# State products of a unit issued ahead of its score products, and the state sum taken in the same unit

## Chip, cores and metric

The kernel runs on one core of one Trainium2 chip. The metric is device time in microseconds of one execution. A core has five engines with queues of their own that run in order: TensorE (PE in the profile, with its weight loads listed as PEld), VectorE (DVE), ScalarE (ACT), GpSimd (POOL) and SyncE (SP, which here only starts DMAs).

## The reference, cut to what matters

A gated recurrence over 768 steps for 4 batches and 8 heads of width 40, followed by a mixture of 16 experts. Only the recurrence bears on this change:

```python
for t in range(S):
    m_new = np.maximum(f_gate[:, :, t] + m, i_gate[:, :, t])
    f_stab = np.exp(f_gate[:, :, t] + m - m_new)
    i_stab = np.exp(i_gate[:, :, t] - m_new)
    m = m_new
    C = f_stab * C + i_stab * outer(v_t, k_t)      # state, per batch and head 40 x 40
    n = f_stab * n + i_stab * k_t
    h_tilde = C @ q_t
    y[:, :, t] = sigmoid(o_t) * h_tilde / max(|n . q_t|, 1)
# then: x = y as rows of 320; a group and an expert chosen per row; out = weight * relu(x w1) w2
```

## The kernel before, in words

**Units.** The recurrence is done in chunks of 128 steps. A unit `u` is one batch in one chunk: `c, b = divmod(u, 4)`, 24 units in all, six chunks. Within a unit the outputs are a sum of two parts: the part from inside the chunk (scores of keys against queries, weighted by a decay, times values) and the part carried in from earlier chunks (queries times the state `Cst`). The state of a batch is kept in SBUF, as four pairs of heads with 41 columns each (40 of the value and one for the normalizer), in `Cst` (also seen as `Cflat`).

**The steps of a unit and their engines:**

- `scores` (L212, PE): 8 products into the two score banks `sp`, in row tiles of 64 and 40 partitions.
- `masked` (L217, DVE): scores times decay, twice, into `pt`.
- `carried` (L237, PE): 8 products of queries and `Cflat` into the tile `it`; nothing in the first chunk. `it` is two banks of PSUM and there is only one buffer of it, so the tile of one unit is given out once all readers of the last unit's are done.
- `carried2` (L244, DVE): reads that part out of `it` into `num`.
- `decayed` (L263, POOL): multiplies the batch's state by the decay of the chunk. Not in the first and last chunk.
- `values` (L284, PE): 8 products of `pt` and the values into `av`.
- `state` (L256, PE): 8 products of weighted keys `kw` and the values, 41 columns each, in column tiles of 64, into the second bank of `it`. Not in the last chunk (units 20 to 23).
- `state2` (L271, in the first chunk L273; DVE): adds these into `Cst`, or copies them.
- `keyw` (L224, POOL): makes `kw` of the next unit from its keys and the last column of its decay.
- `decay` (L182, L185 on PE into `aw`, then four exponentials L195 on ACT into `ab`), in two halves for the unit after the next; `mask` (L166, POOL) of the next unit's decay.
- `norm1`, `rows` (L290 to L300, DVE), `rows2` (L306, POOL), `turn` (L314 on PE, L334 on ACT), `store` (a DMA on SP): normalize the last unit's output, transpose it and store it.

**The order.** Up to unit 21 the order of instructions on each engine is that of the program, written out by hand in `unit(u)`; from unit 22 on a planner orders them by its own costs. In `unit(u)` the small steps of the routing ("chores", `route`, L381 to L452) and the splitting of the first expert's weights into two parts (L651 on ACT, L653 on DVE) are strewn into the later half of a unit. Units with `u % 4 == 0` and `u > 0` also carry the routing logits of the last chunk (`logits_of`, L363 and L368 on PE, L365 on ACT between them), behind `values` and `state`.

The start is written out as well: unit 0 step by step, then `unit(1, first=True)`, in which both halves of the decay of unit 2 follow the scores of unit 1. `gate_sums(1)` (L899 to L923) prepares the gates of the second chunk, mostly on DVE; three steps of it run within unit 0 and the rest behind unit 1. `ends` (L935 on PE, L938 on ACT) follows unit 2; `gate_o` (L163, ACT) is a long activation in units 2, 6, 10 and so on.

Of the kernel before, what the change touches and what calls it, by code (L numbers as in the profile page):

```python
# [7 lines left out]
F32 = mybir.dt.float32  # L8
# [10 lines left out]
P = 128  # L19
# [13 lines left out]
D1 = D + 1  # L33
Z = 64 - D
KS = 64 + D
HC = 4 * D1
# [17 lines left out]
def bc(ap, shape):  # L54
    return ap.broadcast_to(list(shape))
# [3 lines left out]
def lstm_moe(ctx: ExitStack, tc: tile.TileContext, gates, qkT, nat, og, wcat, w1, w2, cst, out):  # L59
    nc = tc.nc  # L60
    enter = ctx.enter_context
    mm = nc.tensor.matmul
# [55 lines left out]
    ps_a = att.enter_context(tc.tile_pool(name="ps_a", bufs=1, space=PSUM))  # L118
# [28 lines left out]
    st_ = {}  # L147
# [9 lines left out]
    def load_o(c):  # L157
        t = wk.tile([P, B, DM], F32, name="sig")
        nc.sync.dma_start(t, og[:, c * B:(c + 1) * B, :])
        sigs[c] = t  # L160
# [36 lines left out]
    def decay(u, r, **kw):  # L197
        aprod(u, r, **kw)
        exps(u, r)
# [14 lines left out]
    def masked(u, r):  # L214
        t = st_[u]
        pt = wk.tile([P, 4, P], F32, name="pt", bufs=4)
        nc.vector.tensor_tensor(pt, t["pm"][r], t["ab"][:, r], op=ALU.mult)  # L217
        t["pm"][r] = pt

    def keyw(u):  # L220
        t = st_[u]
        if u // B < NCH - 1:
# [2 lines left out]
                                    t["nt"][:, DM + H:].rearrange("p (j r d) -> p r j d", r=2, d=D),  # L225
                                    bc(t["ab"][:, :, :, P - 1:P], (P, 2, 4, D)), op=ALU.mult)

    def carried(u):
        c, b = divmod(u, B)
        t = st_[u]  # L230
        it = t["it"] = ps_a.tile([P, 2, 512], F32, name="it")
        if c > 0:
            for pr in range(4):
                for r in range(2):
                    rs = rows_of[r]
                    o = (b * 4 + pr) * D1
                    mm(it[:, r, pr * D1:pr * D1 + P], t["qk"][rs, 1, pr, :], Cflat[rs, o:o + P], start=True, stop=True)  # L237
# [11 lines left out]
    def state(u):  # L249
        c, b = divmod(u, B)  # L250
        t = st_[u]
        nt = t["nt"]
        if c < NCH - 1:
            for j in range(H):
                pr, r0 = j // 2, 64 * (j % 2)
                mm(t["it"][r0:r0 + 64, 1, HC + pr * D1:HC + (pr + 1) * D1], t["kw"][:, pr * KS + r0:pr * KS + r0 + 64],  # L256
                   nt[:, j * D1:(j + 1) * D1], start=True, stop=True)

    def decayed(u):
# [5 lines left out]
    def state2(u):  # L265
        c, b = divmod(u, B)
        if c < NCH - 1:
            st = st_[u]["it"][:, 1, HC:2 * HC].rearrange("p (a e) -> p a e", e=D1)
            cb = Cst[:, b * 4:b * 4 + 4, :]
            if c > 0:  # L270
                nc.vector.tensor_tensor(cb, cb, st, op=ALU.add)  # L271
            else:
                nc.vector.tensor_copy(cb, st)  # L273
# [93 lines left out]
    def logits_back(c):  # L367
        nc.tensor.transpose(out=rt["bank"][:, 0:P], in_=rt["lT"], identity=ident)  # L368
        chores.append([route(c, 0, B, rt["bank"]), "B"])
# [85 lines left out]
    def go_on(n=1, slot=None):  # L455
        while n and chores and slot in (None, chores[0][1]):
            n -= 1
            with ExitStack() as st:
                if not rt["manual"]:
                    st.enter_context(tc.high_priority())  # L460
                chores[0][1] = next(chores[0][0], None)
                if chores[0][1] is None:
                    chores.pop(0)
# [17 lines left out]
    def first_tokens():  # L481
        none = rt["rows"][0]
        nc.sync.dma_start(itab[0:NE * NBLK, :].rearrange("(p a) b -> p (a b)", p=P), none)
        nc.sync.dma_start(itab[NE * NBLK:NE * NBLK + 1, :], none[0:1, 0:P])

    def last_rows():
        zero = rt["rows"][1]
        for b in range(B):
            nc.sync.dma_start(x_d[b * S + S - P:(b + 1) * S, :], zero)
        nc.sync.dma_start(x_d[NTOK:NTOK + 1, :], zero[0:1])  # L490

    def put_id():
        if ids:
            sl, tk = ids.pop(0)
            nc.gpsimd.memset(sep, 0.0)
            no_order("ids", nc.gpsimd.indirect_dma_start(  # L496
                out=itab_flat, out_offset=bass.IndirectOffsetOnAxis(ap=sl, axis=0), in_=tk, in_offset=None))
# [324 lines left out]
    def run(stage, u):  # L822
        if 0 <= u < NU:
            stage(u)
# [12 lines left out]
    def unit(u, more=0, first=False):  # L837
        run(loads, u + 3)
        if u == 6:
            first_tokens()  # L840
        if u == 9:
            last_rows()
        if u % B == 1 and u // B + 1 < NCH:
            load_o(u // B + 1)
        with ExitStack() as st:
            if u == MANUAL:
                st.enter_context(tc.issue_after(rt["av", u - 1].ins))
            run(scores, u)
        if first:
            decay(2, 0)  # L850
            decay(2, 1, pool=ps_1, tag="lg")
        run(norm1, u - 1)
        run(rows, u - 1)
        run(state2, u - 1)
        if u == 21:
            go_on(4, "B")
        run(rows2, u - 1)
        run(store, u - 1)
        run(mask, u + 1)
        run(lambda v: masked(v, 0), u)  # L860
        run(lambda v: masked(v, 1), u)
        run(carried, u)
        run(decayed, u)
        run(carried2, u)
        run(keyw, u + 1)
        run(lambda v: decay(v, 0), u + 2)
        run(turn, u - 1)
        go_on(9, "A")
        if u == 21:
            go_on(3, "B")  # L870
            for _ in range(B):
                put_id()
        if u == 5:
            first_rows()
        if u > NU - 2:
            run(logits, u - 2)
        run(values, u)
        run(state, u)
        if u % B == 0 and 0 < u < NU:
            logits_of(u // B - 1)  # L880
        run(lambda v: decay(v, 1), u + 2)
        if u == NU - 2:
            chores.append([early_counts(), "B"])
        if u < MANUAL:
            go_on(4 + more, "B")
        if u % B == 0 and 0 < u < NU:
            logits_back(u // B - 1)
        if u % B == 2 and u // B + 1 < NCH:
            gate_o(u // B + 1)
        for _ in range(1 if u < 20 else 3):  # L890
            put_id()
# [81 lines left out]
    def sum_on(n=1):  # L973
        for _ in range(n):
            if sums and next(sums[0], StopIteration) is StopIteration:
                sums.pop(0)

    with tc.manual_schedule():
        nc.sync.dma_start(G[:, 0], gates[0:BH])
        nc.scalar.dma_start(cs, cst)  # L980
        nc.scalar.dma_start(G[:, 1], gates[BH:2 * BH])
        nc.scalar.dma_start(G4, gates[2 * BH:])
        nc.vector.memset(ones_b, 1.0)
        nc.vector.memset(sep, 0.0)
        nc.scalar.activation(sep, sep, AF.Exp)
        busy(11)
        nc.vector.memset(ones4, 1.0)
        nc.vector.memset(Dl[:, 0, 0:1], 0.0)
        nc.vector.memset(Apc[96:P], 0.0)
        for t in qkp[0:2]:  # L990
            nc.gpsimd.memset(t[0:Z], 0.0)
        load_qk(0)
        loads(0)
        load_o(0)
        load_qk(1)
        loads(1)
        loads(2)
        nc.scalar.copy(sel_b, cs[:, C_SEL:C_SEL + B * H])
        nc.scalar.copy(lt_b, cs[:, C_LT:C_LT + P])
        nc.scalar.activation(neg_b, ident, AF.Copy, scale=NEG)  # L1000
        sums.append(gate_sums(0))
        sum_on(9)
        for t in kws:
            nc.gpsimd.memset(t, 0.0)
        for t in qkp[2:]:
            nc.gpsimd.memset(t[0:Z], 0.0)
        nc.gpsimd.memset(Cflat, 0.0)
        nc.gpsimd.tensor_copy(id_b, ident)
        decay(0, 0)
        decay(0, 1, pool=ps_1, tag="lg")  # L1010
        scores(0)
        keyw(0)
        masked(0, 0)
        masked(0, 1)
        carried(0)
        carried2(0)
        sums.append(gate_sums(1))
        decay(1, 0)
        values(0)
        gate_o(0)  # L1020
        decay(1, 1, pool=ps_1, tag="lg")
        state(0)
        sum_on(3)
        keyw(1)
        nc.gpsimd.iota(tokid, pattern=[[P, NBLK]], base=0, channel_multiplier=1)
        nc.gpsimd.tensor_copy(keyb, cs[:, C_15E:C_15E + NE])
        nc.gpsimd.tensor_copy(base_b, cs[:, C_BASE:C_BASE + NE])
        nc.gpsimd.memset(ohsum[0], 0.0)
        loads(3)
        nc.sync.dma_start(wc, wcat)  # L1030
        unit(1, first=True)
        sum_on(9)
        sums.append(later_sums())
        sum_on(1)
        for u in range(2, 10):
            unit(u)
            do(due if u in (2, 6) else [])
            sum_on({2: 2, 3: 3, 4: 2, 5: 9}.get(u, 0))
# [211 lines left out]
```

## Time and profile before

| | |
|---|---|
| runs, us | 400.91, 398.45, 399.18 |
| median, us | 399.18 |
| profiled execution, us | 398.51 |
| its span in the trace, us | 396.9 |
| mean granted TensorE clock | 0.981 |
| first score products of unit 0, unit 1, unit 4, unit 20 | 7.26, 12.29, 30.06 and 125.64 us |
| the recurrence ends, the experts begin | about 160 us |

The profile's page gives busy times of engines, the span in 40 slices of 9.9 us, and the chain of work that ended last. The timeline lists instructions in order of time, neighbours of the same kind merged: start, length, engine, line, operation, output and inputs, count, and in square brackets idle time of the engine before it with what ended it. A product in float32 is two records on PE and two weight loads on PEld, so the 8 products of a step appear as x16.

### The profile page before, as it was taken

Reading aid. Unit: us, or ns where it says so; the run is one execution under the profiler, and the core shown is the slowest. Engines: PE = TensorE matmul, PEld = TensorE weight load, DVE = VectorE, ACT = ScalarE, POOL = GpSimd, SP = SyncE. Lnnn points to the kernel's source line nnn. Section 1 sums busy time; section 2 is a strip of 40 time slices with the busy share of each in tenths; the row PEclk is TensorE's granted clock in tenths of the full one; section 3 lists DMA queues with packets and bytes.
Section 4 is the critical chain, followed back from the end, with each engine's and each line's share of the span. In section 5 each row is a group of like instructions: output and inputs, shape, how many; then the busy total and the mean of one; then the engine's idle time right before and its main releaser. Section 6 shows DMA issues by size and latency. Waiting matters only on the chain.

```text
span 396.9 us, 9817 instructions
## 1 busy us (share of the span) xinstructions
PE 379.4 (96%) x3673; PEld 349.4 (88%) x3673; DVE 267.0 (67%) x702; ACT 212.8 (54%) x544; POOL 175.0 (44%) x231
## 2 busy tenths in 40 slices
PE   8989999999999977999999999999999999999994
PEld 4778998889899866799999998999999998888994
DVE  4777777998888944874957768756745666555520
ACT  5765565666656501625655566656655645445520
POOL 7445576476675544356432206352142315232310
PEclk9999999999999988699999999999999999999999
DMA  7976559999898217029951369996664537887700
GB/s 235 274 225 207 156 80 308 269 322 228 190 304 152 88 23 215 3 61 335 411 207 53 112 250 362 414 310 232 248 226 151 185 110 253 318 307 269 282 18 10
DMA packets 28340, 83.38 MB, mean 210 GB/s; under 512 B 11463, under 2 KB 15550, under 8 KB 24708
## 3 DMA queue, kind: packets, MB, share of 16 engines
q1 hardware_dynamic: 22724, 64.74, 52.1%
q0 software_dynamic: 5232, 17.65, 13.2%
q8 instruction: 29, 0.48, 0.5%
q10 hardware_dynamic: 336, 0.36, 0.3%
q14 instruction: 19, 0.16, 0.2%
HBM read 72.97 MB, written 9.99 MB: 209 GB/s over the span
## 4 chain that ended last, share of the span: by engine, by line
PE 71%; issue 8%; DVE 8%; DMA 7%; POOL 2%; ACT 1%; POOLq 1%; DVEq 0%; SPq 0%; ACTq 0%
PE psh L768 11%; PE av L284 10%; PE psh L736 6%; PE po L796 5%; PE po L798 5%; PE po L797 5%; PE sp L212 5%; PE it L237 4%; DMA itab<-tokid,slot 3%; PE aw L185 3%; PE it L256 2%; PE tpm L314 2%; PE po L788 2%; DMA w1s<-in_w_dram 2%; PE busy L127 2%
## 5 line engine op out<-in xcount | busy, mean ns | idle before, releaser
L195 ACT ACTIVATE ab<-aw,bcol 128x128 f32<-128x128 f32 x192 | 54.6, 371 | 38.0 <-PE aw L185 36.1
L592 POOL DMA_INDIRECT out_dram<-y,ix x32 | 36.1, 1128 | 70.3 <-ACT y L808 61.8
L588 POOL DMA_INDIRECT xg<-x_d,ix x32 | 35.8, 1119 | 64.7 <-DMA ix<-itab 40.0
L796 PE MATMUL po<-w2h,hh 128*128 128x320 f32 (+3 forms) x200 | 63.1, 316 | 0.8 <-ACT hh L722 0.8
L798 PE MATMUL po<-w2h,hh 128*128 128x320 f32 (+3 forms) x200 | 61.9, 310 | 0.0
L797 PE MATMUL po<-w2l,hh 128*128 128x320 f32 (+3 forms) x200 | 61.7, 309 | 0.0
L768 PE MATMUL psh<-xhl,w1hl 128*128 128x256 f32 (+5 forms) x336 | 53.9, 290 | 0.9 <-ACT xhl L696 0.4
L653 DVE TENSOR_TENSOR w2l<-w2s,w2h 128x640 fp32r<-128x640 f32 x52 | 41.0, 818 | 17.2 <-ACT w2h L651 17.1
L284 PE MATMUL av<-nt,pt 128*128 128x128 f32 x384 | 49.1, 283 | 2.3 <-DVE pt L217 2.3
L284 PEld LDWEIGHTS av<-nt,pt 128*128 128x128 f32 x384 | 46.3, 197 | 3.2 <-DVE pt L217 3.2
L768 PEld LDWEIGHTS psh<-xhl,w1hl 128*128 128x128 f32 x336 | 46.7, 193 | 1.9 <-PE psh L768 0.8
L722 ACT ACTIVATE hh<-psh 128x256 fp32r<-128x256 f32 (+5 forms) x68 | 29.1, 431 | 35.3 <-DVE hf L720 17.6
L736 PEld LDWEIGHTS psh<-xhl,w1s 128*128 128x128 f32 x336 | 40.9, 191 | 2.9 <-ACT y L808 2.1
L736 PE MATMUL psh<-xhl,w1s 128*128 128x144 f32 (+3 forms) x336 | 42.5, 285 | 0.2
L725 DVE SCALAR_TENSOR_TENSOR hh<-psh,hh 128x256 fp32r<-128x256 f32 (+4 forms) x76 | 32.7, 445 | 14.7 <-ACT hh L722 13.7
L217 DVE TENSOR_TENSOR pt<-sp,ab 128x512 f32<-128x512 f32 x48 | 30.9, 686 | 14.6 <-PE sp L212 11.3
L808 ACT ACTIVATE y<-po,xg 128x320 f32<-128x320 f32 (+3 forms) x25 | 13.2, 529 | 49.5 <-PE po L798 48.6
L796 PEld LDWEIGHTS po<-w2h,hh 128*128 128x128 f32 (+3 forms) x200 | 36.5, 182 | 2.2 <-ACT hh L722 1.1
L798 PEld LDWEIGHTS po<-w2h,hh 128*128 128x128 f32 (+3 forms) x200 | 36.4, 182 | 0.2
L797 PEld LDWEIGHTS po<-w2l,hh 128*128 128x128 f32 (+3 forms) x200 | 36.4, 182 | 0.0
L651 ACT CAST w2h<-w2s 128x640 fp32r<-128x640 f32 x52 | 35.1, 725 | 0.9 <-DMA w2s<-in_w_dram 0.9
L496 POOL DMA_INDIRECT itab<-tokid,slot x24 | 27.1, 1129 | 16.6 <-DVE slot L430 6.6
(217 smaller groups left out, 733.0 us busy)
## 6 DMA issues: line engine op xcount, KB each, us to landing
w1s<-in_w_dram SPq DMA_DIRECT2D x12, 1536.0 KB, 8.1
w2s<-in_w_dram SPq DMA_DIRECT2D x9, 1280.0 KB, 9.4
nt<-in_nat_dram SPq DMA_DIRECT2D x24, 324.0 KB, 6.4
qk<-in_qkT_dram SPq DMA_DIRECT2D x24, 320.0 KB, 7.5
x_d<-x SPq DMA_DIRECT2D x24, 192.0 KB, 5.9
sig<-in_og_dram SPq DMA_DIRECT2D x6, 640.0 KB, 8.2
w1hl<-in_w_dram SPq DMA_DIRECT2D x3, 1280.0 KB, 10.1
w1s<-in_w_dram SPq DMA_DIRECT2D x4, 768.0 KB, 7.2
```

Source lines behind the costliest of these rows:

```text
L195: rt["exp"] = nc.scalar.activation(st_[u]["ab"][:, r, j, :], aw[:, j, :], AF.Exp, bias=bcol[:, c, i:i + 1])
L284: ins = mm(av[:, i:i + P], t["pm"][r][:, pr, :], nt[:, o:o + P], start=True, stop=True)
L588: return nc.gpsimd.indirect_dma_start(out=o, out_offset=None, in_=src, in_offset=bass.IndirectOffsetOnAxis(ap=idx, axis=0))
L592: return nc.gpsimd.indirect_dma_start(out=out, out_offset=bass.IndirectOffsetOnAxis(ap=idx, axis=0), in_=y, in_offset=None, bounds_check=N ...
L651: nc.scalar.copy(a, src[:, s])
L653: lows.append(lambda: nc.vector.tensor_tensor(o[rows], src[rows, s], a[rows].bitcast(F32), op=ALU.subtract))
L725: nc.vector.scalar_tensor_tensor(hh[:, f:f + per, dst], src[:, :, t], 0.0, hr.bitcast(F32)[:, :, t], op0=ALU.max, op1=ALU.subtract)
L736: ins = mm(ps[:, g * W1:(g + 1) * W1], w1s[:, s], xhl[:, k, :], start=(k == 0), stop=(k == 2))
L768: ins = mm(ps[:, g * W1:(g + 1) * W1], w[:, s], x, start=(n == 0), stop=(n == len(todo) - 1))
L796: mm(po[0:m], hh[:, f, t], w2h[:, s], start=st0, stop=False)
L797: mm(po[0:m], hh[:, f, t], w2l[:, s], start=False, stop=False)
L798: ins = mm(po[0:m], hh[:, f, tl], w2h[:, s], start=False, stop=sp0)
```

## The change

In a unit, `state(u)` moves from behind `values(u)` to ahead of `scores(u)`. `state2(u)` moves from the next unit (behind `rows`) to its own unit, behind `carried2(u)`. The tile `it` is given out by whichever of `state` and `carried` comes first, and the state products go to columns 256 to 419 of its second bank in place of 164 to 327, because `carried` now writes columns 0 to 250 after them. In unit 0 `state` stays where it is and `state2(0)` follows it at once.

```diff
+    def inner(u):
+        if "it" not in st_[u]:
+            st_[u]["it"] = ps_a.tile([P, 2, 512], F32, name="it")
+        return st_[u]["it"]
+
     def carried(u):
         c, b = divmod(u, B)
         t = st_[u]
-        it = t["it"] = ps_a.tile([P, 2, 512], F32, name="it")
+        it = inner(u)
...
-                mm(t["it"][r0:r0 + 64, 1, HC + pr * D1:HC + (pr + 1) * D1], t["kw"][:, pr * KS + r0:pr * KS + r0 + 64],
+                mm(inner(u)[r0:r0 + 64, 1, 2 * P + pr * D1:2 * P + (pr + 1) * D1], t["kw"][:, pr * KS + r0:pr * KS + r0 + 64],
                    nt[:, j * D1:(j + 1) * D1], start=True, stop=True)
...
-            st = st_[u]["it"][:, 1, HC:2 * HC].rearrange("p (a e) -> p a e", e=D1)
+            st = st_[u]["it"][:, 1, 2 * P:2 * P + HC].rearrange("p (a e) -> p a e", e=D1)
...
         if u % B == 1 and u // B + 1 < NCH:
             load_o(u // B + 1)
+        run(state, u)
         with ExitStack() as st:
...
             run(scores, u)
...
         run(norm1, u - 1)
         run(rows, u - 1)
-        run(state2, u - 1)
...
         run(carried, u)
         run(decayed, u)
         run(carried2, u)
+        run(state2, u)
         run(keyw, u + 1)
...
         run(values, u)
-        run(state, u)
...
         decay(1, 1, pool=ps_1, tag="lg")
         state(0)
+        state2(0)
         sum_on(3)
         keyw(1)
```

## The prediction

> **What bounds the kernel now.** I read the page first: busy times, the slices, the chain.
>
> ```profile
> span 396.9 us, 9817 instructions
> ...
> PE 379.4 (96%) x3673; PEld 349.4 (88%) x3673; DVE 267.0 (67%) x702; ACT 212.8 (54%) x544; POOL 175.0 (44%) x231
> ...
> PE   8989999999999977999999999999999999999994
> ...
> PEclk9999999999999988699999999999999999999999
> ...
> PE 71%; issue 8%; DVE 8%; DMA 7%; POOL 2%; ACT 1%; POOLq 1%; DVEq 0%; SPq 0%; ACTq 0%
> ```
>
> TensorE carries the chain, and no slice of the recurrence (the first 13, up to 129 us) shows it much under nine tenths. So a step that only moves on PE's queue is worth what it changes in waits and in the change-over from one kind of product to the next. The tile `it`, the one that moves, comes next: who reads it, and who waits for it.
>
> ```profile
> L271 DVE TENSOR_TENSOR Cflat<-Cflat,it x16: 318/318/320, 36.0 to 126.2; 128x164 f32<-128x164 f32 x16
> ...
> who waited for it (us, times):
>   PEld it L237: 1.5, 3
> ```
>
> The wait that the move of the sum takes away (`carried` held up by the last unit's `state2`) is 1.5 us in three places, in a kernel of 397. Next the weight loads of unit 15, a plain unit, which show PE's cycle without gaps:
>
> ```profile
> 96.41 0.97 PEld L212 LDWEIGHTS sp<-qk 64*128 64x128 f32 x16
> ...
> 98.97 1.86 PEld L284 LDWEIGHTS av<-nt,pt 128*128 128x128 f32 x16
> 100.96 0.55 PEld L256 LDWEIGHTS it<-nt,kw 128*64 128x64 f32 x16
> 101.56 0.23 PEld L185 LDWEIGHTS <-sel_b 128*128 128x128 bf16 x4
> 101.89 0.97 PEld L212 LDWEIGHTS sp<-qk 64*128 64x128 f32 x16
> ```
>
> From `values` to `state` 1.99 us, from `state` to the decay product 0.60, from that to the next scores 0.33: 2.92 from `values` to `scores`.
>
> **The change, part by part.**
>
> *The order on PE in a plain unit.* The new order is `values`, decay product, `state`, `scores`. Unit 21 has no `state`, and shows what `values` costs ahead of a decay product; the start of unit 1 shows `state` straight ahead of `scores`.
>
> ```profile
> 135.20 1.86 PEld L284 LDWEIGHTS av<-nt,pt 128*128 128x128 f32 x16
> 136.99 0.32 PEld L185 LDWEIGHTS <-sel_b 128*128 128x128 bf16 x4
> ```
>
> ```profile
> 11.69 0.55 PEld L256 LDWEIGHTS it<-nt,kw 128*64 128x64 f32 x16
> 12.29 0.97 PEld L212 LDWEIGHTS sp<-qk 64*128 64x128 f32 x16
> ```
>
> `values` then takes 1.79 instead of 1.99, `state` 0.60 as before. The decay product ahead of `state` is not shown in a plain unit; below nothing it can't be, as the load ahead needs its 0.23, and ahead of the row tiles of `scores` it takes 0.33: I take 0.33. Sum 1.79 + 0.33 + 0.60 = 2.72, **0.20 us less per plain boundary**. In units 4, 8, 12 and 16 the logits' products, in column tiles of 32, follow `values` directly and keep the 1.99: nothing saved. Behind unit 19 the boundary also loses `state` itself, since unit 20 has none: 0.80 less. That 0.60 is paid at the start, where unit 1's products now come ahead of its scores.
>
> *The start.* Before, `state(1)` ran behind `values(1)`, long after its `kw`. Now it stands at 12.29 in PE's queue, and POOL has no `kw` yet:
>
> ```profile
> 13.27 0.74 POOL L224 TENSOR_TENSOR kw<-nt,ab 128x320 f32<-128x320 f32 x1 [2.49 <-DMA nt<-in_nat_dram]
> ...
> 15.23 0.42 PEld L185 LDWEIGHTS <-sel_b 128*128 128x128 bf16 x4 [0.91 <-issue]
> ...
> 15.89 1.86 PEld L284 LDWEIGHTS av<-nt,pt 128*128 128x128 f32 x16
> ...
> 26.46 0.34 ACT L938 COPY decs<-tp 64x16 f32<-64x16 f32 x2
> ...
> 26.87 0.31 PEld L314 LDWEIGHTS tp<-cs,x 128*128 128x128 f32 x3 [1.18 <-POOL ab L166]
> ```
>
> `kw` is ready at 14.01; with the 0.07 that a release takes (26.80 to 26.87 in the last two rows), `state(1)` starts at 14.08, `scores(1)` at 14.68 instead of 12.29: **2.39 us late**. Queued behind the waiting products are the scores, both decay products of unit 2, with them ACT's exponentials, and so all of unit 1. No other work fills the gap. At `scores(2)` the first 0.20 is back: 2.19. In unit 3 PE already idles 1.18 us ahead of `turn`. The profile names POOL there; but the copy that frees the tile ends at 26.80 on ACT, and PE goes on at 26.87. That copy stands in ACT's queue behind exponentials which wait for a decay product, and this product no longer has `state` and its change-over ahead of it (0.80). So `turn` comes 2.19 - 0.80 = 1.39 late, and part of the stall is swallowed by an old gap. PE's own arrival (26.87 - 1.18 + 1.99 = 27.68) is ahead of that (28.26). `scores(4)`: 1.39 - 0.20 = **1.19 us late**.
>
> The copy `state2(0)` now waits on DVE for `state(0)`, with six gate sums behind it:
>
> ```profile
> 9.75 0.51 DVE L899 TENSOR_TENSOR_SCAN M__125<-G,M__125 32x128 f32<-32x128 f32 x1
> ...
> 11.92 0.28 DVE L907 TENSOR_TENSOR G<-G,A__128 32x128 f32<-32x128 f32 x1
> ```
>
> These 2.45 us move from 9.75 to about 12.8, and `norm1(0)` and the masks of unit 1 behind them end near 17.4. What hides it is the stall on PE: unit 1's `values`, at 15.89 before, start at 18.3. Nothing added; without that cover it would be up to 2 us more.
>
> *The sum of states on DVE.* From the place between `rows` and `masked` it takes away 0.24 us (79.05 to 79.29 below). But in its own unit it must wait for `decayed` on POOL, where the normalization of the last rows and the mask of the next decay go first. Unit 12, where `carried` waited longest:
>
> ```profile
> 78.70 0.44 DVE L300 SCALAR_TENSOR_TENSOR xn<-sig,av 128x320 f32<-128x320 f32 x1
> ...
> 79.05 0.32 DVE L271 TENSOR_TENSOR Cflat<-Cflat,it 128x164 f32<-128x164 f32 x1
> 79.23 0.71 POOL L306 TENSOR_TENSOR x<-xn,den 128x320 f32<-128x320 f32 x1 [1.21 <-DVE xn L300]
> 79.29 1.28 DVE L217 TENSOR_TENSOR pt<-sp,ab 128x512 f32<-128x512 f32 x2
> 79.42 0.97 PEld L237 LDWEIGHTS it<-Cflat,qk 64*128 64x128 f32 x16 [0.79 <-DVE Cflat L271]
> ...
> 80.96 0.45 POOL L263 TENSOR_TENSOR Cflat<-Cflat,decs 128x164 f32<-128x164 f32 x1
> 80.98 1.86 PEld L284 LDWEIGHTS av<-nt,pt 128*128 128x128 f32 x16
> ...
> 81.05 0.40 DVE L447 TENSOR_TENSOR sg<-sm,oh 128x16 f32<-128x16 f32 x1
> ...
> 81.38 0.73 POOL L224 TENSOR_TENSOR kw<-nt,ab 128x320 f32<-128x320 f32 x1
> ```
>
> `decayed` ends at 81.41; the sum follows at about 81.46, and the first chore at 81.70 instead of 81.05: 0.65 us later, counted from the same `xn`. Behind the waiting sum stand the unit's chores and weight splits, then `norm1`, `rows`, and with them `x`, `turn` and the next `pt`. Where DVE has room this costs nothing; where it has none, its loop from one `xn` to the next grows by 0.65. Room by unit:
>
> ```profile
> 60.83:66.19 5.36, 5.36 (x76) 4.97 (x75) 3.77 (x12) 2.51 (x10) 3.63 (x6) 1.00 1.08 251
> ...
> 72.01:77.67 5.66, 5.63 (x77) 5.04 (x76) 5.19 (x22) 3.95 (x11) 3.79 (x7) 1.00 0.92 269
> 77.67:85.07 7.40, 6.75 (x102) 5.78 (x101) 7.11 (x17) 5.23 (x15) 5.14 (x7) 1.00 1.04 335
> 85.07:90.59 5.52, 5.52 (x76) 5.04 (x75) 4.98 (x16) 2.63 (x10) 3.93 (x6) 1.00 1.05 305
> ```
>
> (columns: stretch, length, busy PE, PEld, DVE, ACT, POOL). Unit 9 has 1.6 us of DVE idle: free. Units 11 and 12 have 0.47 and 0.29: +0.18 and +0.36, together +0.5. Unit 13 has 0.54, about what the loop needs. I read 10, 14, 16 and 17, with chores or splits as well, by it, and take it that they just give back what PE would gain, the removed wait of `carried` among it: what is late there next is `x` for `turn`, or `pt` for `values`, as both hang on `xn`.
>
> The Trainium skill speaks here too ("SBUF — State Buffer", Who interferes with whom): a VectorE instruction with two inputs from SBUF fully blocks against a GpSimd instruction that reads SBUF. The trace bears it out, since the small L447 takes 0.40 us beside `decayed`; the sum reads PSUM for one input, keeps 318 to 320 ns, and is not slowed. By this rule some of the 0.65 is not lost, as the first chore would have had to sit out `kw` anyway; the sum would come out by some tenths lower.
>
> *The rest.* The moved steps start no DMA and pass none. `state`'s new wait for `kw` has room: in unit 12 `kw` ends at 82.11, while `values`, started at 80.98, is over at 82.77 and the logits come first. From unit 22 on nothing in the program changes, so I let the shift pass through.
>
> **The sum**, against the profiled 398.51 us (span 396.9 and 1.6 around it): start +1.19; units 5, 6, 7, 9, 15 and 18, 6 x 0.20 = -1.2; behind unit 19 -0.8; units 11 and 12 +0.5. Total -0.3, so 398.2 for that execution; it lies 0.7 under the median of 399.18, so **398.9 us** as a median. Ends: if all eleven plain boundaries gain 0.20, the 1.5 us of waits go too and DVE costs nothing, 1.2 - 2.2 - 0.8 - 1.5 = -3.3; if seven loaded units each lose the full 0.65, 1.2 - 1.2 - 0.8 + 4.6 = +3.8.
>
> **The rivals.**
>
> *PE stays the bound throughout* (395.9). For it: PE is busy in 5.52 of 5.52 us even in unit 13. Against: DVE's rows of units 11 and 12.
>
> *DVE's loop is the bound in all loaded units* (half to full price, 401 to 403). For it: the loop now runs through POOL's queue once per unit. Against: unit 13 shows 0.54 us of idle on DVE.
>
> *The clock drops at the start* (slower). PE idles 1.79 us ahead of `state(1)`, in one piece. Late in the recurrence just such a gap ends in slow products:
>
> ```profile
> 135.23 2.03 PE L284 MATMUL av<-nt,pt 128*128 128x128 f32 x16
> ...
> 142.71 3.61 PE L284 MATMUL av<-nt,pt 128*128 128x128 f32 x16 [1.79 <-DVE pt L217]
> ...
> 143.00:160.00 17.00, 14.54 (x113) 13.16 (x113) 8.18 (x36) 1.70 (x5) 6.77 (x9) 0.80 0.43 127
> ```
>
> The same step took 3.61 instead of 2.03, and the granted clock (third column from the right) over these 17 us was 0.80. A time at half speed costs half its length; at 0.80 that is 6.8 slow us and 3.4 lost in this stretch. At the start, 1.6 to 5 us more than the sum: 400.5 to 404, with 402.5 in the middle. It decides from the point where the gap, with what idles around it, fills enough of the stretch by which the clock is set; the gap of 0.91 us ahead of 15.23 did no harm. The Trainium skill ("TensorE: Matmul & The Clock Gate", What's actually happening) asks for a whole idle window of about 3.4 us; by that rule the new gap does nothing. The row with 1.79 us differs, so the rival keeps a chance.
>
> *The later part goes another way* (397 or 401): the planner orders units 22, 23 and the experts by its own reckoning of when engines come free, and that has moved; nothing in the trace speaks for a side.
>
> **How the numbers follow.** Forecast (-0.3, give or take 1.5: 397.4 to 400.4) 0.54; PE the bound 0.14; DVE's loop 0.12; the clock 0.08; the later part 0.12. The range leaves out the outer part of each side rival: 396.0 to 402.2. A measurement here tells about 1% (4 us, 395.2 and 403.2) from no change. Faster than that: four tenths of the first rival and a little of the last, 0.08; slower: parts of the clock, DVE and late rivals, 0.08; the same 0.84.
>
> **What would show it.** In the new trace: PE idle ahead of L256 near 12.3 us with `kw` as its end, `scores(1)` near 14.7 and `scores(4)` near 31.2; boundaries of 2.72 in plain units; `carried` straight behind the loads of `scores` everywhere; `state2` behind `decayed`, and units 11 to 13 longer or no shorter. Then `scores(20)` within a microsecond and a half of 125.3. I am wrong if the stall at the start is not there, if DVE's chores cost nothing, or if the part behind 126 us changes by itself.

## The result, and the profile after

The changed kernel came out slower than forecast in the first comparison: 402.75 us median (6 runs) beside 400.05 us for the kernel before, ratio 1.0107 [1.0067, 1.0147], against a forecast of 398.9 beside 399.18 (0.9993). Two later comparisons of the same kernel, on two chips, gave 398.02 beside 396.32 us, ratio 1.0040 [1.0011, 1.0068], and 395.56 beside 395.04 us, ratio 1.0004 [0.9983, 1.0025], 12 runs each. So the loss is clear of the noise in two of three, and not of one size. Ratios here are between undisturbed runs, so they need not be the quotients of the medians (the first leaves out 404.86 and 404.32 us of the six runs of before), and of the kernel with a later gate only the part of the profile ahead of 126 us is used, as it was disturbed behind that.

The page of the changed kernel's profiled execution (402.42 us) answers to that of before as follows.

```profile
span 400.8 us, 9816 instructions
...
PE 377.3 (94%) x3673; PEld 349.2 (87%) x3673; DVE 264.5 (66%) x702; ACT 213.5 (53%) x544; POOL 173.4 (43%) x231
...
PE   8899999989999796899999999999999999999994
...
PEclk9899999999999998699899999999999999999999
...
PE 63%; DVE 11%; issue 10%; DMA 7%; POOL 5%; ACT 2%; POOLq 1%; SPq 0%; DVEq 0%
```

TensorE is busy for 2 us less in a span that is 4 us longer. On the chain, 8 points went from PE to DVE, POOL and issue. The clock row has two new dents, in the second slice and in the twentieth.

The start, from the timeline, and then busy time and granted clock (third column from the right) in stretches of 3.41 us:

```profile
12.87 0.73 POOL L224 TENSOR_TENSOR kw<-nt,ab 128x320 f32<-128x320 f32 x1 [2.31 <-ACT ab L195]
13.66 0.55 PEld L261 LDWEIGHTS it<-nt,kw 128*64 128x64 f32 x16 [1.62 <-POOL kw L224]
14.26 1.73 PE L212 MATMUL sp<-qk 64*128 64x128 f32 x16
```

```profile
11.26:14.68 3.42, 1.92 (x43) 1.64 (x43) 2.31 (x6) 1.14 (x4) 1.23 (x5) 1.00 1.05 253
14.68:18.09 3.41, 3.13 (x24) 2.19 (x21) 3.15 (x12) 1.09 (x5) 0.72 (x1) 0.50 1.08 249
...
188.76:192.17 3.41, 1.62 (x11) 1.17 (x10) 3.07 (x7) 3.41 (x8) 0.00 (x0) 1.00 1.01 382
192.17:195.58 3.41, 3.41 (x16) 3.39 (x15) 3.22 (x4) 2.62 (x6) 1.43 (x2) 0.50 1.03 420
```

`state(1)` does wait for `kw(1)`. Then the 3.41 us from 14.68 run at half speed, and the scores of unit 1 take 1.73 us instead of 1.16.

Who makes the sum of states wait in its new place (all of the changed kernel), and unit 12 in order of time:

```profile
L276 DVE TENSOR_TENSOR Cflat<-Cflat,it x16: 313/326/326, 35.0 to 124.8; 128x164 f32<-128x164 f32 x16
its engine sat idle before it (us, times) until:
  POOL Cflat L268: 5.4, 9
```

```profile
80.58 0.44 DVE L305 SCALAR_TENSOR_TENSOR xn<-sig,av 128x320 f32<-128x320 f32 x1
...
81.80 1.05 ACT L656 CAST w1hl<-w1s 128x1024 fp32r<-128x1024 f32 x1 [1.91 <-DMA w1s<-in_w_dram]
...
82.85 0.45 POOL L268 TENSOR_TENSOR Cflat<-Cflat,decs 128x164 f32<-128x164 f32 x1
...
83.33 0.33 DVE L276 TENSOR_TENSOR Cflat<-Cflat,it 128x164 f32<-128x164 f32 x1 [0.71 <-POOL Cflat L268]
83.57 0.45 DVE L452 TENSOR_TENSOR sg<-sm,oh 128x16 f32<-128x16 f32 x1
```

The first chore starts 2.99 us behind `xn`, where it was 2.35 before: 0.64 later, as worked out. A plain boundary, that of unit 9, and the end of unit 19:

```profile
64.61 1.86 PEld L289 LDWEIGHTS av<-nt,pt 128*128 128x128 f32 x16
66.39 0.32 PEld L185 LDWEIGHTS <-sel_b 128*128 128x128 bf16 x4
66.82 0.55 PEld L261 LDWEIGHTS it<-nt,kw 128*64 128x64 f32 x16
67.41 0.75 PEld L212 LDWEIGHTS sp<-qk 64*128 64x128 f32 x12
```

```profile
123.73 1.27 ACT L163 ACTIVATE sig<-sig 128x1280 f32<-128x1280 f32 x1 [1.74 <-DMA sig<-in_og_dram]
...
126.86 0.38 PE L185 MATMUL aw<-Apc,sel_b 128*128 128x128 bf16 x4 [0.96 <-ACT ab L195]
```

The boundary takes 1.78 + 0.43 + 0.59 = 2.80 us. At the end of unit 19 there is something that the prediction did not have: the gate's tanh waits for its transfer, ACT's exponentials stand behind it, and PE behind these.

The table compares each profiled execution with that of the kernel before, counted from its own scores(0), in microseconds (negative is earlier or shorter). The start of scores is the first weight load of the unit's scores in the timeline. Before, the stretches are 22.80 (scores(0) to scores(4)), 47.61 (units 4 to 11), 7.40, 35.12, 5.45 and, from scores(20) to the end of the span, 271.3.

| | start | units 4 to 11 | unit 12 | 13 to 18 | unit 19 | sum at scores(20) | scores(20) to end |
|---|---|---|---|---|---|---|---|
| forecast | +1.19 | -0.62 | +0.36 | -0.40 | -0.80 | -0.27 | 0 |
| changed, first | +2.25 | -1.41 | +1.07 | -0.55 | +0.38 | +1.74 | +2.4 |
| changed, second | +2.22 | -1.43 | +0.86 | -0.39 | +1.20 | +2.46 | -1.9 |
| changed, third | +2.49 | -1.42 | +0.52 | -0.05 | -0.79 | +0.75 | -3.6 |
| state(1) alone ahead | +3.37 | -0.01 | -0.01 | 0.00 | -0.01 | +3.34 | -1.3 |
| old start | -0.21 | -1.42 | +1.04 | -0.56 | -0.79 | -1.94 | +0.4 |
| old start, again | -0.21 | -1.32 | +0.46 | -0.09 | -0.35 | -1.51 | -1.8 |
| gap filled | +1.30 | -1.42 | +1.01 | -0.55 | +0.85 | +1.19 | -1.3 |
| decay a unit ahead | +1.74 | -1.30 | -0.08 | -1.11 | -0.79 | -1.54 | +1.2 |
| gate later | +1.18 | -1.42 | +0.97 | -0.52 | -0.79 | -0.58 | not used |
| order on PE alone | -0.92 | -0.77 | -0.02 | -0.19 | -0.01 | -1.91 | -3.0 |
| both repairs | -0.21 | -1.42 | +2.36 | -1.55 | -0.80 | -1.62 | -2.4 |
| both, cast later | -0.21 | -1.30 | -0.08 | -0.46 | -0.79 | -2.84 | -1.1 |
| both, cast and gate later | -0.39 | -1.34 | -0.07 | -0.47 | -0.79 | -3.06 | +1.1 |

The last column spreads over 6 us (267.6 to 273.7 us from scores(20) to the end): the three executions of one and the same kernel have +2.4, -1.9 and -3.6. The order of instructions in that part is the same on all five engines as before, but for the sum of unit 19, which now stands ahead of it. Much of the spread goes with the chip: the four executions on one chip took 268.3 to 269.5 us there, the four on another 270.0 to 272.4, the two used on a third 270.2 and 272.3, the one on a fourth 267.6, and the kernel before has its medians in much the same order on these chips (396.32, 398.49, 398.94 and 395.04 us). So single profiles are compared here up to scores(20), and the whole by the ratios to the runs of the kernel before beside them.

### The profile page after: what moved, and what is told of

It is laid out like the page before. It is cut to its first block, busy times and chain, and to the rows that moved or that the text cites. A ratio compares the mean times of both kernels' runs of the same rounds, so it can differ in the third digit from the quotient of the medians.

```text
span 400.8 us, 9816 instructions
## 1 busy us (share of the span) xinstructions
PE 377.3 (94%) x3673; PEld 349.2 (87%) x3673; DVE 264.5 (66%) x702; ACT 213.5 (53%) x544; POOL 173.4 (43%) x231
## 4 chain that ended last, share of the span: by engine, by line
PE 63%; DVE 11%; issue 10%; DMA 7%; POOL 5%; ACT 2%; POOLq 1%; SPq 0%; DVEq 0%
PE psh L773 13%; PE psh L741 6%; PE po L801 6%; PE po L803 6%; PE po L802 6%; PE av L289 5%; PE sp L212 3%; PE tpm L319 3%; DMA nt<-in_nat_dram 2%; PE po L793 2%; DMA x_d<-x 2%; PE it L261 2%; PE aw L185 2%; PE it L242 2%; DMA w2s<-in_w_dram 2%
## 5 line engine op out<-in xcount | busy, mean ns | idle before, releaser
L773 PE MATMUL psh<-xhl,w1hl 128*128 128x256 f32 (+5 forms) x336 | 54.9, 294 | 0.9 <-ACT xhl L701 0.4
L773 PEld LDWEIGHTS psh<-xhl,w1hl 128*128 128x128 f32 x336 | 48.0, 197 | 1.7 <-PE psh L773 0.8
L289 PE MATMUL av<-nt,pt 128*128 128x128 f32 x384 | 47.6, 277 | 1.0 <-DVE pt L217 1.0
L289 PEld LDWEIGHTS av<-nt,pt 128*128 128x128 f32 x384 | 44.7, 192 | 1.9 <-DVE pt L217 1.9
```

What stands on the lines that cost most here:

```text
L289: ins = mm(av[:, i:i + P], t["pm"][r][:, pr, :], nt[:, o:o + P], start=True, stop=True)
L773: ins = mm(ps[:, g * W1:(g + 1) * W1], w[:, s], x, start=(n == 0), stop=(n == len(todo) - 1))
```

## The experiments

Three theories were tried. START: the loss is the stall ahead of `state(1)` and the slow clock behind it. LOOP: it is the sum of states that waits behind `decayed` on POOL. LATE: it is the part behind 130 us.

**Old start.** In units 0 and 1 `state` stays in the old order, the sum of unit 0 returns to unit 1, and the sum of unit 1 follows at the end of that unit; the rest is the changed kernel.

```diff
-        run(state, u)
+        if u != 1:
+            run(state, u)
...
         run(values, u)
+        if u == 1:
+            state(1)
...
```

> The changed kernel, but the first two units keep the old order: state(1) behind values(1), the sums of units 0 and 1 where they stood. Theory START (most of the loss is the stall and the half-speed clock behind it, 2.25 us at scores(4), and the late losses follow from that lateness): scores(4) back at 30.0 to 30.2 instead of 32.1, no half-speed stretch near 14.7 us, and a time of 397.5 to 399.5, level with the kernel before or a little under it. Theory LOOP (the sum of states behind decayed on POOL costs in units 10 to 21, and the late part inherits it): scores(4) back as well, but unit 12 still takes 8.3 to 8.5 us, and the time stays at 400.5 to 401.5. Theory LATE (the part behind 130 us answers to any shift in its own way): the time can't be had from the early part; the gaps near 134, 161 and 192 us stay or go by themselves.

397.74 beside 398.49 us, ratio 0.9968 [0.9935, 1.0001]. scores(4) is back at 29.73, the half-speed stretch at 15 us is gone, and unit 12 still takes 8.44 us. The early part is as both said, and a little earlier; unit 12 is as LOOP said; the time goes with START.

> The changed kernel with units 0 and 1 in the old order, a second time, beside the others of this call. Theory START: ratio 0.994 to 1.000 again, 3 to 5 us under the changed kernel; theory LATE: it differs from the first time by more than 0.6%.

396.19 beside 396.32 us, ratio 1.0004 [0.9977, 1.0030], on the chip on which the changed kernel had 1.0040. The changed kernel there was 1.8 us slower, less than START named (3 to 5 us), and the two intervals overlap: the times alone don't prove the repair, the profiles do up to scores(20).

**state(1) alone ahead.** The kernel before, with `state(1)` ahead of `scores(1)` and the sum of unit 0 in its own unit. The sum of unit 1, which the expectation names too, stays in unit 2 here.

```diff
+        if u == 1:
+            state(1)
...
             run(scores, u)
...
-        run(state2, u - 1)
+        if u != 1:
+            run(state2, u - 1)
...
-        run(state, u)
+        if u != 1:
+            run(state, u)
...
         state(0)
+        state2(0)
```

> The kernel before, with unit 1's state products alone moved ahead of its scores, and the sums of units 0 and 1 in their own units. Theory START: kw(1) holds PE as in the changed kernel, half-speed clock near 14.7 us, scores(4) at 31.9 to 32.3, and the lateness runs through to the end: 400.5 to 402.5, most of the 1% lost. Theory LOOP: scores(4) late by about 2, but the loaded units 10 to 14, where DVE is the bound, take part of it back, and the end is within 1 us of the kernel before. Theory LATE: the gap between 130 and 200 us differs from both kernels.

400.77 beside 398.49 us, ratio 1.0051 [1.0014, 1.0087]. Here the transfer of `nt` came later, and the gap fell into one stretch of the clock:

```profile
13.86 0.73 POOL L224 TENSOR_TENSOR kw<-nt,ab 128x320 f32<-128x320 f32 x1 [3.20 <-DMA nt<-in_nat_dram]
14.65 0.55 PEld L261 LDWEIGHTS it<-nt,kw 128*64 128x64 f32 x16 [2.49 <-POOL kw L224]
15.24 1.78 PE L212 MATMUL sp<-qk 64*128 64x128 f32 x16
```

```profile
12.21:15.62 3.41, 1.03 (x25) 0.92 (x24) 3.02 (x11) 1.43 (x5) 1.19 (x5) 1.00 1.06 254
15.62:19.03 3.41, 3.23 (x25) 2.29 (x23) 2.33 (x7) 1.00 (x4) 0.72 (x1) 0.50 1.05 271
```

Counted from the start of the span, the lateness at scores(4), 3.28 us, is 3.25 at scores(20): no unit from 4 on takes any of it back. In this kernel the start alone costs half a per cent, with PE idle for 2.49 us ahead of `state(1)` in the profiled execution, where the changed kernel had 1.62.

**Gap filled.** The changed kernel, with seven products of ones ahead of `state(1)`.

```diff
+        if first:
+            busy(7)
         run(state, u)
```

> The changed kernel, with seven idle-time products of ones on PE ahead of state(1), so that PE does not stand still while it waits for kw. If the idle gap of 1.8 us is what brings the half-speed clock at 14.7 us: no half-speed stretch there, scores(1) takes 1.16 us and not 1.73, scores(4) at about 31.2 instead of 32.1, and the time 0.5 to 1 us under the changed kernel. If the drop has another cause: the same 3.4 us at half speed, scores(4) at 32.1 or later, and no gain.

```profile
13.70:17.11 3.41, 3.24 (x45) 2.30 (x44) 3.24 (x11) 0.57 (x3) 1.50 (x6) 1.00 1.06 257
10.29:13.70 3.41, 3.41 (x39) 2.54 (x39) 0.90 (x3) 2.46 (x6) 0.62 (x2) 1.00 1.04 260
```

398.91 beside 398.49 us, ratio 1.0011 [0.9968, 1.0054]. The wait for `kw` is still there, the half-speed stretch is not; scores(1) takes 1.16 us, and the start costs 1.30 instead of 2.25. So the drop was worth 0.95 us in the early part, and it went with the idle gap. One execution alone doesn't show the cause, as two without the filling escaped the drop too (below); that the idle share of a stretch brings it rests on the stretches of all profiles, in the last section. The expected gain in time over the changed kernel can't be read, as that has no runs beside these.

**Decay a unit ahead.** The changed kernel, with `decayed(u + 1)` queued on POOL behind `keyw(u + 1)` in unit u and written to a second buffer, so that it needn't wait for `carried`.

```diff
-            nc.gpsimd.tensor_tensor(cb, cb, bc(decs[:, c, b * 4:b * 4 + 4].unsqueeze(2), (P, 4, D1)), op=ALU.mult)
+            nc.gpsimd.tensor_tensor(Cdec[:, b * 4:b * 4 + 4, :], cb, bc(decs[:, c, b * 4:b * 4 + 4].unsqueeze(2), (P, 4, D1)), op=ALU.mult)
...
-                nc.vector.tensor_tensor(cb, cb, st, op=ALU.add)
+                nc.vector.tensor_tensor(cb, Cdec[:, b * 4:b * 4 + 4, :], st, op=ALU.add)
...
-        run(decayed, u)
...
         run(keyw, u + 1)
+        run(decayed, u + 1)
```

> The changed kernel, with the decay of the states on POOL written into a second buffer and queued a unit ahead, so that the sum of states on DVE waits for no POOL work of its own unit. Theory LOOP: the waits of the sum for POOL (9 of them, 5.4 us) go, unit 12 falls from 8.47 to about 7.4 us, scores(20) comes 1.0 to 1.5 us earlier than in the changed kernel, and the time 1 to 2.5 us under it. Theory START: unit by unit little changes (at most 0.5 us at scores(20)), and the time stays within 0.7 us of the changed kernel, 401.5 to 403.

398.51 beside 398.49 us, ratio 0.9988 [0.9954, 1.0022].

```profile
L277 DVE TENSOR_TENSOR Cflat<-Cdec,it x16: 312/314/315, 35.0 to 122.6; 128x164 f32<-128x164 f32 x16
its engine sat idle before it (us, times) until:
who waited for it (us, times):
```

```profile
10.27:13.68 3.41, 2.38 (x34) 2.03 (x32) 0.88 (x3) 2.46 (x6) 0.32 (x1) 1.00 1.04 257
13.68:17.10 3.42, 2.46 (x40) 2.05 (x41) 3.24 (x11) 0.12 (x1) 1.88 (x6) 1.00 1.06 264
```

All waits of the sum are gone, unit 12 falls to 7.32 us, and units 13 to 18 are shorter as well. LOOP's mechanism is there, and its price is 1.7 us over units 12 to 18: together they are at -1.19 here, and at +0.52, +0.47 and +0.47 in the three executions of the changed kernel. At scores(20) the gain on the first of these is 3.3 us, more than LOOP's 1.0 to 1.5; 1.2 of it is unit 19 and 0.5 the start. The start had a stall of 2.11 us, longer than in the changed kernel, but the gap straddles two stretches of the clock: 2.38 and 2.46 us busy of 3.41, and neither was followed by half speed.

**The changed kernel again.**

> The changed kernel once more, to see which of its late losses come back and how large the loss is beside the kernels tried here. Theory START (a stall of 1.6 to 2.5 us ahead of state(1), and a half-speed stretch behind it where that gap falls into one of the clock's 3.41 us stretches; the late parts answer to chance): 399.5 to 401.5, ratio 1.002 to 1.007, the gaps at 161 and 192 us and the half-speed stretch at 192 us mostly gone. Theory LATE (the late loss belongs to the program): ratio 1.009 to 1.014 again, half-speed stretch near 192 us again.

Ratio 1.0040 [1.0011, 1.0068]: as START said, though the time, 398.02 us, is under its range on this chip. The half-speed stretch at 15 us came back, that at 192 did not; the gate's tanh waited even longer, and unit 19 took 6.65 us:

```profile
124.51 1.27 ACT L163 ACTIVATE sig<-sig 128x1280 f32<-128x1280 f32 x1 [2.56 <-DMA sig<-in_og_dram]
```

> The changed kernel a third time. The first comparison gave 1.0107 [1.0067, 1.0147] from 6 runs, the second 1.0040 [1.0011, 1.0068] from 12. Theory START and LOOP (2 to 2.5 us late at scores(20) in most executions, less where the gap at the start straddles two of the clock's stretches or the transfer of sig is in time): 1.002 to 1.008; scores(4) at 31.4 to 32.2, with the half-speed stretch at 15 us only if PE's busy share in the stretch ahead of it is under six tenths. Theory LATE: 1.009 or more, with a half-speed stretch behind 170 us again.

Ratio 1.0004 [0.9983, 1.0025], under both. The start was late again (scores(4) at 32.74, with half speed behind 1.9 us busy of 3.4), but the tanh waited for nothing, unit 19 took 4.66 us, and the part behind scores(20) was the shortest of all. LATE, as a property of the program, falls: neither repeat has the half-speed stretch at 192 us, and this ratio is far under LATE's 1.009.

**Gate later.** The changed kernel, with the tanh one unit later on ACT.

```diff
-        if u % B == 2 and u // B + 1 < NCH:
+        if u % B == 3 and u // B + 1 < NCH:
             gate_o(u // B + 1)
```

> The changed kernel, with the gate's tanh of the next four units queued on ACT one unit later. In the changed kernel it waited 1.7 and 2.6 us for its transfer behind unit 18 and held up the exponentials behind it, and unit 19 came out 0.4 to 1.2 us longer than before instead of 0.8 shorter. If that wait is the whole of it: no wait for sig, unit 19 at 4.6 to 4.9 us (before 5.45, changed 5.83), scores(20) 1.0 to 1.8 us earlier than in the changed kernel, and a time 0.3 to 1.5 us lower, ratio to the kernel before 0.999 to 1.004. If something else makes unit 19 long (the wait of the sum behind POOL): unit 19 stays at 5.4 or more.

400.93 beside 398.94 us, ratio 1.0034 [0.9998, 1.0069]. Unit 19 takes 4.66 us, and there is no half-speed stretch at the start, so scores(20) is at -0.58, as near to the forecast as any. The time doesn't show it: the gain was 1.3 to 3.0 us at scores(20) and is not in the ratio. Where it went is not shown.

**Order on PE alone.** The kernel before, with `state` behind the decay product of its unit and ahead of the next scores. The sum stays where it was, and so does unit 1.

```diff
         run(values, u)
-        run(state, u)
...
         run(lambda v: decay(v, 1), u + 2)
+        run(state, u)
```

> The kernel before, with the state products alone moved behind the decay product of their unit (ahead of the next unit's scores); the sum of states stays in the next unit and unit 1 stays as it was. This is the new order on PE without the new place of the sum on DVE. Theory CHANGE-OVER (the order on PE saves 0.11 us in a plain boundary and 0.7 to 0.8 in unit 3): scores(4) 0.3 to 0.8 us earlier than before, scores(12) 0.7 to 1.8 earlier, no loss of 1 us in unit 12, a time 0.5 to 2 us under the kernel before (ratio 0.995 to 0.999). Rival: carried waits longer for the sum of states, which now comes later because state does: the waits of carried grow from 1.5 us in 3 places to 3 us or more, and the time is that of the kernel before.

394.82 beside 396.32 us, ratio 0.9971 [0.9946, 0.9997]. It went as CHANGE-OVER said: scores(4) 0.92 us earlier, a little more than expected, scores(12) 1.69, unit 12 at 7.38 us. The rival, `carried` waiting twice as long, did not:

```profile
  PEld it L237: 1.8, 4
```

(waits of `carried` for the sum, 1.5 us in 3 places before). In units 12 to 17 the order on PE is worth nothing. DVE sets their length: up to unit 15 its loop from one `xn` to the next is the same as before to 0.01 us.

**Both repairs**, old start and decay a unit ahead.

> Both repairs in the changed kernel: units 0 and 1 in the old order, and the decay of the states on POOL in a second buffer a unit ahead. If the two losses add up: scores(4) at 29.7, scores(12) at 75.9, unit 12 at 7.3 to 7.4 us, scores(20) at 122.0 to 123.5 (before 125.64), and a time of 395.5 to 397.5, ratio 0.990 to 0.996. If DVE's loop or the part behind 130 us swallows it: level with the start repair alone, 397 to 398.5, ratio 0.996 to 1.0.

393.36 beside 396.32 us, ratio 0.9917 [0.9890, 0.9945]: faster than either kernel. Unit 12 fell out of line, at 9.76 us, so that scores(20) came at 123.92 and not at 122.0 to 123.5:

```profile
80.99 1.05 ACT L657 CAST w1hl<-w1s 128x1024 fp32r<-128x1024 f32 x1 [2.41 <-DMA w1s<-in_w_dram]
...
83.65 0.57 PEld L369 LDWEIGHTS lg<-xT,wc 128*32 128x32 f32 x18 [2.33 <-ACT xT L340]
```

A weight cast waits on ACT for its transfer, and the copy for the logits stands behind it. So the cast was moved.

```diff
-            do(early_splits, {11: 2, 13: 1, 14: 1, 15: 1, 17: 1, 18: 1}.get(u, 0))
+            do(early_splits, {11: 1, 12: 1, 13: 1, 14: 1, 15: 1, 17: 1, 18: 1}.get(u, 0))
```

> Both repairs, and the second of the two weight casts on ACT behind unit 11 moved behind unit 12. With both repairs alone unit 12 took 9.76 us, as a cast waited 2.41 us for its weights on ACT ahead of the copy that the logits need. If that wait is the cause: unit 12 at 7.2 to 7.6 us, scores(13) at 83.1 to 83.6 (both repairs alone: 85.70), scores(20) 1 to 2.3 us earlier, a time 0.5 to 2 us under both repairs alone, ratio 0.986 to 0.992. If DVE's loop takes it back later: unit 12 short, but scores(20) within 0.5 us of 123.9.

396.22 beside 398.94 us, ratio 0.9934 [0.9901, 0.9967]. Unit 12 takes 7.32 us and scores(20) is 1.2 us earlier than with both repairs alone, as expected; but the ratio, on another chip, is no lower, and misses the expected 0.986 to 0.992.

> The same with the gate's tanh one unit later as well. With both repairs the transfer was there in time, so no change: within 0.4% of the kernel without it. A gain would show that the wait for sig comes and goes between executions.

396.38 beside 398.94 us, ratio 0.9950 [0.9916, 0.9985]: no change from the kernel above, as expected. What moving the cast gained ahead of scores(20) (1.2 us over both repairs alone) did not show in either ratio.

## Why the prediction was wrong

**Where the miss lies.** The forecast for the profiled execution was 398.2 us, and it took 402.42. Of these 4.2 us the table has 2.0 ahead of scores(20): the start is 1.06 over its term, unit 12 0.71 and unit 19 1.18, while units 4 to 11 and 13 to 18 are 0.94 under theirs. Another 2.4 us lie behind scores(20) and did not come back in the other two executions of this kernel. Of these losses only the start's is about the same in all three.

**The start.** The stall was right: counted from scores(0), scores(1) is 2.18 us late (7.21 beside 5.03), 2.39 forecast. The step that failed is its price: the sum took the gap at its bare length, +1.19, and left "the clock drops at the start" as a rival at 0.08. The term came out at +2.22 to +2.49 in the three executions of the changed kernel. The drop came in four of the six executions that have the stall and no filling, and cost about 1 us; with the gap filled the term was +1.30. The reason against it was the row with 0.91 us of gap that did no harm; the row that pointed the right way was the other one quoted there, with 1.79 us.

That the term was +1.18 with the gate later, where the clock held, is in part luck. Unit 3 was to give back 1.00 us of the stall, and in the changed kernel it gave back 0.70, with PE still idle for 0.59 us ahead of `turn`. In the two kernels with a later gate that idle time is gone, and unit 3 gave back 0.88: there the tanh of unit 2 no longer stands on ACT ahead of the copy that frees the tile for `turn`. That it was this copy, and not POOL, was read rightly.

**The plain boundary.** Forecast 2.72 us, measured 2.80: the decay product between two float32 steps takes 0.43 to the next load, not the 0.33 taken from its place ahead of `scores`. So 0.12 saved, not 0.20. Units 4 to 11 gained 1.41 all the same. Unit 11, counted as a loss of 0.18, gained 0.40 on PE (its loss on DVE shows in unit 12, below). Unit 7 gained 0.44: an old gap ahead of `turn` went, which the timeline of before has and the prediction overlooked.

```profile
51.02 0.31 PEld L314 LDWEIGHTS tp<-cs,x 128*128 128x128 f32 x3 [0.29 <-issue]
```

Unit 7 gained as much with the order on PE alone. Units 13 to 18 came near their term (-0.55, forecast -0.40) by luck: units 15 and 18, which were to give it, came out at +0.01 and +0.12, and unit 17 gave 0.51.

**The sum of states.** The wait behind `decayed` was sized right (0.64 measured, 0.65 forecast) and the place was right, but its price was too low. DVE's loop shows it, from `xn` in unit 11 over unit 12 to unit 13, before and changed:

```profile
72.48 0.44 DVE L300 SCALAR_TENSOR_TENSOR xn<-sig,av 128x320 f32<-128x320 f32 x1
78.70 0.44 DVE L300 SCALAR_TENSOR_TENSOR xn<-sig,av 128x320 f32<-128x320 f32 x1
82.08 2.35 DVE L653 TENSOR_TENSOR w1hl<-w1s,w1hl 128x1024 fp32r<-128x1024 f32 x2
84.35 0.50 DVE L290 TENSOR_TENSOR av<-av,num 128x328 f32<-128x328 f32 x1
85.40 0.43 DVE L300 SCALAR_TENSOR_TENSOR xn<-sig,av 128x320 f32<-128x320 f32 x1
```

```profile
73.88 0.44 DVE L305 SCALAR_TENSOR_TENSOR xn<-sig,av 128x320 f32<-128x320 f32 x1
80.58 0.44 DVE L305 SCALAR_TENSOR_TENSOR xn<-sig,av 128x320 f32<-128x320 f32 x1
87.70 0.44 DVE L305 SCALAR_TENSOR_TENSOR xn<-sig,av 128x320 f32<-128x320 f32 x1
```

The loop grew from 6.22 to 6.70 us in unit 11 and from 6.70 to 7.12 in unit 12: +0.48 and +0.42, where +0.18 and +0.36 were forecast. It is the same to 0.02 us in all seven profiles that have the wait, and 6.40 and 6.66 with the decay a unit ahead. The idle 0.47 and 0.29 us of DVE were taken as room that the wait could fill; only 0.16 and 0.22 were. In unit 12 the late weights' difference already ran right up to the next `norm1` before the change (82.08 to 84.43, `norm1` at 84.35), so the idle time was no gap at that place.

On PE both losses show in unit 12, 0.5 to 1.1 us of it. The cast that waits for its transfer on ACT in the rows of unit 12 is not the cause: with the gap filled it waited for no transfer, and unit 12 took 8.42 us all the same.

**Behind unit 19.** The 0.80 came in full where the tanh did not wait for the transfer of `sig` (-0.79 or -0.80 in seven executions, two of them with the gate later), and turned into up to 1.20 of loss where it did: with waits of 1.01, 1.74, 2.21 and 2.56 us unit 19 took 5.10, 5.83, 6.30 and 6.65 us. The prediction followed PE's queue there and not ACT's, where a tanh of 1.27 us stands ahead of the exponentials; the old profile had the hint:

```profile
121.65 1.27 ACT L163 ACTIVATE sig<-sig 128x1280 f32<-128x1280 f32 x1 [0.20 <-DMA sig<-in_og_dram]
```

From issue to landing this transfer took 14.1 us before, 15.6 in the second execution of the changed kernel and 12.9 in the third. Why it varies is not shown.

**From unit 22 on** "the shift passes through" holds for the program, as its order is unchanged, and not for an execution: the rest of the span varies by 6 us. The first comparison had a second half-speed stretch at 192 us, ahead of which PE was busy for 1.62 us of 3.41, and its rest was 2.4 us longer; the third had 3.6 us less. A change by itself behind 126 us was one of the prediction's own signs of being wrong; but the planner's order, the reason given for that rival, did not change. Why the three comparisons spread from 1.0004 to 1.0107, wider than their intervals, stays open; chip and clock stretches are candidates that were not separated.

**The rivals.** PE the bound throughout: no, units 11 and 12 grew with DVE's loop. DVE's loop the bound in all loaded units, at half to full price: no, units 11 and 12 pay 0.90 us together, and units 12 to 18 as a whole come out 0.5 us longer than before. The two losses hid a gain that the forecast had not seen: the three kernels with both repaired are 0.5 to 0.8% faster than before.

## What to carry to other kernels

When a step moves ahead in one queue, check the first pass of the loop by itself: there its input may not be ready, and what was free in the steady state becomes a stall, and here no unit behind the first four gave any of it back. When a reader moves close behind its writer on another engine, count what stands ahead of that writer in its queue, and free the pair with a second buffer before judging the order. A gap on TensorE cost more than its length here when it left a clock stretch about half idle, and with a few filler products in the gap that price was not paid.

## What was not expected of the hardware

Half-speed stretches last 3.41 us or a multiple of it. Laid out in steps of that length from its first half-speed stretch, each execution has its own grid. Over the 14 profiled executions, as far as they are used here, all 16 stretches at full speed in which PE was busy for less than half were followed by half speed. Between 0.51 and 0.67 it went both ways (6 of 24), and above that none of 1411 was. That fits the start, where a gap of 1.6 to 2.5 us brought the drop in some executions and not in others: 0.30 to 0.56 of the stretch was busy ahead of the four drops, 0.70 or more in the two executions without one. At 0.56, three of these drops lie where it can go either way. The Trainium skill ("TensorE: Matmul & The Clock Gate", What's actually happening) describes a free-running window of this length, and the traces agree. Its table there asks for an idle window before the clock falls; the traces differ, as 1.92 us busy of 3.42 was enough.

With the decay a unit ahead, POOL's product ran beside the weights' difference on DVE:

```profile
83.11 1.54 POOL L269 TENSOR_TENSOR Cdec<-Cflat,decs 128x164 f32<-128x164 f32 x1
83.12 2.61 DVE L659 TENSOR_TENSOR w1hl<-w1s,w1hl 128x1024 fp32r<-128x1024 f32 x2
```

1.54 us instead of 0.45, and 2.61 instead of 2.36. By the Trainium skill ("SBUF — State Buffer", Who interferes with whom) such a pair shares a port under an exclusive lock, which agrees. Nobody waits for that product here; whether the 0.25 us more on DVE costs anything is not shown.
